# Token-mixing second weights loaded in two pieces, and the hand-kept instruction order replaced, in a two-layer attention and MLP kernel

## The chip, the cores and the metric

The kernel runs on one core of a Trainium2 chip. The metric is the device time of one execution in microseconds (us). TensorE (PE in the profile, its weight loads PEld), VectorE (DVE), ScalarE (ACT) and GpSimd (POOL) compute, SyncE (SP) issues nearly all DMAs. Every engine takes its own instructions strictly in the order in which they are written, and waits at semaphores for the others.

## The reference, cut to what matters

```python
x = x + A(layernorm(x), wqkv, wo)      # S = 2048 tokens, D = 512, 32 heads of 16
x = x + B(layernorm(x), w1, b1, w2, b2)
# both lines once more with the same weights: two layers

def A(x, wqkv, wo):                    # sliding-window attention, window W = 256
    q, k, v = heads(x @ wqkv)
    scores = q @ k.T * 16 ** -0.5, masked to 0 <= query - key < 256
    return softmax(scores) @ v, heads joined, @ wo

def B(x, w1, b1, w2, b2):              # the MLP mixes tokens, not features; F = 1792
    u = gelu(einsum("sd,sf->df", layernorm(x), w1) + b1)
    return transpose(u @ w2 + b2)      # [D, F] @ [F, S]
```

## The kernel before, in words

**Tiling.** x lies in SBUF as 16 tiles of 128 tokens by 512 features. Attention runs over four query blocks of 512 tokens (Q = 0 to 3). For a block, q, k and v are projected (four 128x512 products each, line 526, with the masking copies of lines 537 and 542 behind them), then four groups of heads (t = 0 to 3) with nine steps each (m = 0 to 8) follow. A step is a scores operation on TensorE (`emit_scores`, line 684: 4, 8 or 12 small 64x64 products), an exp on ScalarE (`emit_exp`, line 695), one or two small edge masks on VectorE or GpSimd (line 712), and a product with v (`emit_pv`, line 733, small products again). Probabilities go round through seven slots, the scores through two pairs of PSUM banks. After step 8 the sums are copied out (line 358 on VectorE, 360 on ScalarE) and DMAs bring the denominators together and add the second half of a pair of groups to `oU` (line 755); `job_inverse` and `job_normalise` (lines 757 and 767, a small-tile product at 777) divide, and `job_outproj` (line 648) multiplies with wo and adds to x.

**MLP.** The first product (`u_product`, line 849) runs over 14 tiles of F and 16 token tiles, in groups of four products (line 855). Its parts that need early tokens only are done inside attention. A gelu (line 903) makes the tile of `uT`. The second product (`job_y`, line 906) makes a token tile st of the output out of 14 products of 128x512 (line 928), in two operations of 10 and 4 products with one accumulation, and VectorE adds the result to x (line 932); the last tile of layer 2 is done in two halves of 256 columns (lines 915 and 919). In layer 1 the later of these products are laid between the steps of the second layer's attention; in layer 2 they come last, and each tile's output DMA follows its addition (line 940; 922 for the halves).

**The second weights.** A block s2 of w2 serves two token tiles and is 128 x 14 x 256 in bf16, 896 KB. `w2_dma` (line 845) loads it in one DMA into a home (`w2_place`, line 836): one of two slots of `w1buf`, or one of the two halves of `oU`. The load waits for every reader of the home, and each product waits for the whole block (`held`). Blocks 0 to 3 are loaded at the end of the first product, blocks 4 to 7 when `job_y` has used their home up (lines 935 to 938).

**What sets the order.** Every operation is a `plan.op` with its reads and writes, numbered as it is made. The five strings of `ORDER` give each engine its list of operations, two letters to a number: they fix both the sequence of each engine and, for operations that several engines can do, which does it. `BANKS` gives the PSUM bank (6 or 7) of each product that has no bank of its own. `arrange` (line 151) reads both; `needs` (line 199) works out which semaphores each operation has to wait for. SyncE's DMAs use 16 semaphores in turn, so that a DMA also waits for the one 16 places before it.

Of the kernel before, what the change touches and what calls it, by code (L numbers as in the profile page):

```python
# [29 lines left out]
AuAvAwAxAyAzBLBJA0BPBRBNBTBXBVDTB1CeCuA1A2CjCoBpCyCcC3C9D1A3CnDEDKCxBtC2DODXC8DkDDDeDJDNDmDVDbBxDsDxB5DBD4DiD9DrGsEKECDwEFFZD3EPD8EBEaEJGQEOETEjEeEyEp  # L30
EuGiE3EiE8EoEtFBE2FJE7FOF2FVFAFIFcFEFxFNFSF4HlF9FbGCFwGIF1F8GMGBGTHYGdGHGLGSGWGlICGpGvHLG2GkGoG9G7HCGuG1HGIQHOG5HBHFHVHNHSHeHaHiHrI0HyHdH6HhHqHxH-HuII
H5H+INKmIcIHIMIgIkIoIVIsKUIxIfIjI6JpI-IrIwJVH1JaI5I+JiJCJmJEJuJZJ1JfJyJ6JdKwJlJ+JtJxKLJ5LpKPJ9KXLbKhKKKOKpMFKtKWKaKzK-K6KoLBKsKyK5LGLPLKK9LFLSNILYLJLh
NSLmLRLVLuNLL1LgL9LlLdMCLtL0MKL8MBLxMJMOMPMdNBMlMhMWMpNwMtMgMkMxL4M5MsMwM+NgNEM4M9NNNQNXNDNdMSNKNnNUNtNaN1NcNmN5OOOGNsN0OKO+OTN4OFOJOeOQOXOiOnOpOhOtPm
O0OmO6NqPBOsOzPFM0O5PKPSQYPAPEPfPJPPPZPVPtPYPePjPNP4PyNkPcQAPiPsQHPoPxP3QRP-O3QGQbQKQVQoQkQUQaQfRXP7QvQeQ1Q-Q5QjQuQ0RDORRKQ4Q+RORHQERURcRRRNRhRTRbRgRm
RlRzR0QsSuR3R4R5SxSyS0SrS1SvS3SwSGS6S7SDS4S2SVSJSsSRSNS8S5StSlSmSzSnS9TRTFTBTNTSTHTDTOTdTVThTZTaTeTWSoTiSpSqS-TLTJT1TwT7T2T8UAUBTxUpUOUdUXUZUqUTUVUkU2
UbUeU6UlUiVbUPVMVCVKWdVVVQWeU+VeVjYXVGYYVoVvVUVsXyXzWiVdV0ViV4VnVuVzWAWNV9WPV3V-WHWEWyXRWZWUXAWlWLWqZgXBWvW3WTWYWkXkYrW8WpXNWuZWXWW2W7XGXbX7XgXVXaXfXp
YQXuX4aFYAXoYFXtZvYMX3X-YEYJYTaGYmYta2YyYSYlY3YqYxY8adZHZAa3Y2Y7Y-ZZZGZKZRbgZdZjZEbhZqZxZYcDZ2ZcZiZpZ6Zta-aCaNZ-Z1aaZ5aBaKaWaQaqaVaZajaia8apaxaSa7aybK
cGbFbdcHbZbEbJbSdRbqbucbbybNbcb7blcAambtbxcTb6b-cYdjcgcFcXckatcscdcweNc4cjcrc8bmdJcvc3c7dIdNdMdUb1eZdedmcndTdXdrczdxd4d9dld-dqdwd3eEgAeId7eQemeWeDeHef
duejePeTerfDeze7eeebeifAfIeqeyeufNe6e-fbfHfMfUfffjfngjfrfvfegXf3fifqfuf9e2gDf2gIiDgQf8gCgHgNgUh0gcgggLgogTgbgfgsfQg5gngrg9hchIg4hTfyg8hEhMhXheighChihp
hshthWhwh3hbhhhFh7hohviAiSiIh2h6iPhGiWh-iFiaiTikiOiVipiLiZivijioi3iuidi2i-i+jCjJjQjNkRjTjXjgj4jcjojMiyjujSjWjbjyjnjtjxj8jkj3kDkAkHjlkKkOkWi7kGkbkNkVka  # L40
kgkfktkui8kLkxkykzlrlslulolllmlvlplAl0lxk9l1lylPltlDlzlLlHl2lwlqlnlflglhmBl9l-mLl3mMmbmTmUmHl7mImcmPmQlimXljlkmYl5mFmDmjm1msmkmnmwmom2mxmtm5m6nCm+m-nH
# [25 lines left out]
ABAAACADAIAEAGAHAFCiCwDSCsC7CtDIDWDjGhGgG6EWEnHKEXEZEYGbGaGZGcHRDqK+KlKkGGIZLOIYIaIvIbKTKdKgKeKfMbMZMcMaOaOcOdObOWQNPwQPQnQOQQP2PrRfQiQzRyRkR8R9R+R-Q9
LkOlSjSiRGTuTvSkTlTmUDT4WMV8VZVaXDYaXLXJXKXMZuZ+ZUZVZPZNZOZQbVbYbWbXdid8dheMdpdadbdcddfXfZfYfahPf7hRhShQjGhLjFinjHjIitjahBj2jfkZiihakek4k2k3k5jsleksld
# [29 lines left out]
class Plan:  # L98
# [172 lines left out]
def bass_interleave_layers__sliding_block__mixer_token_mlp__prompt_kernel(  # L271
# [17 lines left out]
    NFT = F // P  # L289
# [5 lines left out]
    with es:  # L295
# [22 lines left out]
        uT = sb("uT", [P, NFT, D])  # L318
# [32 lines left out]
        def load(dst, src, size, prio, **kw):  # L351
            return plan.op({SP: (600, lambda e: e.dma_start(dst, src))}, prio=prio, dma=size, **kw)
# [553 lines left out]
        def job_y(st, b, L, prio):  # L906
            s2, last_layer = st // 2, L == 1
            blk, held = w2_place(L, s2)
            if last_layer and st == NT - 1:
                for h, bank in enumerate((b, b + 1)):  # L910
# [7 lines left out]
                    pe(f, 1530, prio, reads=held + [R("uT", fc) for fc in range(NFT)], writes=[BK(bank)])  # L918
# [6 lines left out]
            for lo, hi in ((0, 10), (10, NFT)):  # L925
                def f(e, lo=lo, hi=hi):
                    for fc in range(lo, hi):
                        r = e.matmul(ps[:, b, :], lhsT=blk[:, fc, (st % 2) * P:(st % 2 + 1) * P],  # L928
                                     rhs=uT[:, fc, :], start=(fc == 0), stop=(fc == NFT - 1))
                    return r  # L930
                pe(f, 217 * (hi - lo), prio, reads=held + [R("uT", fc) for fc in range(lo, hi)], writes=[BK(b)])
# [131 lines left out]
```

## Time and profile before

| | before |
|---|---|
| median of 3 runs (lowest, highest) | 492.09 us (491.19, 492.58) |
| the profiled execution itself | 492.09 us |
| its span, first to last instruction | 490.3 us |
| granted TensorE clock | 1.00 |
| TensorE busy | 467.3 us, 95% of the span |
| ScalarE busy | 319.8 us, 65% |
| VectorE busy | 337.4 us, 69% |
| GpSimd busy | 196.3 us, 40% |
| SyncE DMAs (instructions of `sync`) | 178 |

Stages, as the lines of the timeline show them: layer 1 attention to about 160 us, its first MLP product to 202 us, second MLP product to 224 us and then mixed into the attention of layer 2, which ends at about 396 us; first MLP product to 438 us; second to 488 us.

A row of a group reads: line, engine, operation, written tile <- read tiles, shape, count | busy us, mean ns of one | idle us of the engine just before them and what ended most of it. A row of waits reads: who <- whom: us in total, times, longest us. A row of the timeline reads: start, length, engine, line, operation, count, and in brackets the idle time before it with what ended it. A row of a stretch reads: stretch, its length, then busy us and count for PE, PEld, DVE, ACT and POOL, the clock, the DMA share and GB/s. In the chain a piece reads: start, length, what. "issue" is idle time for which the profile shows no cause.

### The profile page before, as it was taken

To read this page: it belongs to the slowest core of one execution; us is meant where nothing else is said; L and a number is where in the kernel's file an instruction comes from. 1 tells how busy PE (TensorE), PEld (TensorE's weight loads), DVE (VectorE), ACT (ScalarE), POOL (GpSimd) and SP (SyncE) were. 2 spreads that over 40 slices of the span, in tenths; PEclk is the share of its full clock that TensorE was granted. 3 is DMA by queue.
4 is the path that set the end of the run, shared out by engine and by line. 5 is a ranking of instruction groups with operands and counts; after the bars stand their busy time and mean duration, and the time that the engine had idled before them with its cause. 6 is when DMAs were issued, how large, how long until landed. Compare 5 with 4: busy or idle time off the path is not lost.

```text
span 490.3 us, 17141 instructions
## 1 busy us (share of the span) xinstructions
PE 467.3 (95%) x7614; PEld 255.4 (52%) x7706; DVE 337.4 (69%) x710; ACT 319.8 (65%) x391; POOL 196.3 (40%) x362
## 2 busy tenths in 40 slices
PE   8989989999999999999999999999999999999997
PEld 6544555565555444444455555655556544444444
DVE  7999988988878550256878677999978745220214
ACT  5989989999989202404769898989999830440000
POOL 4989886444622210021439253645674220000000
DMA  7533159200105872240116300240020666080833
GB/s 215 100 77 90 40 115 97 70 6 25 50 6 153 237 175 76 75 132 19 31 16 170 51 27 4 39 101 8 24 70 4 197 188 171 0 226 19 228 107 118
DMA packets 83465, 43.58 MB, mean 89 GB/s; under 512 B 18752, under 2 KB 82368, under 8 KB 83392
## 3 DMA queue, kind: packets, MB, share of 16 engines
q1 hardware_dynamic: 79520, 42.48, 33.1%
q0 software_dynamic: 3872, 0.02, 1.8%
q8 instruction: 60, 0.98, 0.9%
q14 instruction: 13, 0.11, 0.1%
HBM read 32.51 MB, written 2.10 MB: 71 GB/s over the span
## 4 chain that ended last, share of the span: by engine, by line
PE 77%; DVE 14%; ACT 4%; issue 3%; POOL 1%; POOLq 0%
PE ps L855 19%; PE ps L928 18%; PE ps L526 12%; PE ps L684 11%; PE ps L733 9%; PE ps L653 4%; ACT p_sb L695 4%; DVE q_sb L537 2%; DVE stats L460 2%; DVE p_sb L712 2%; PE ps L777 1%; DVE v_all L586 1%; DVE x_sb L657 1%; DVE k_sb L537 1%; DVE oU L358 1%
## 5 line engine op out<-in xcount | busy, mean ns | idle before, releaser
L695 ACT ACTIVATE p_sb<-ps 128x1024 bf16<-128x1024 f32 (+8 forms) x288 | 260.8, 973 | 26.0 <-PE ps L684 23.8
L712 POOL TENSOR_TENSOR p_sb<-p_sb,edge 128x128 bf16<-128x128 bf16 (+2 forms) x225 | 107.5, 494 | 122.8 <-ACT p_sb L695 99.0
L684 PE MATMUL ps<-q_sb,k_sb 64*64 64x288 bf16 (+8 forms) x2816 | 106.4, 250 | 2.3 <-issue 1.3
L526 PE MATMUL ps<-xhT,wqkv 128*128 128x512 bf16 x335 | 86.2, 380 | 7.7 <-issue 4.7
L733 PE MATMUL ps<-p_sb,v_all 64*64 64x288 bf16 (+8 forms) x2816 | 89.5, 246 | 1.7 <-DVE oU L358 0.7
L684 PEld LDWEIGHTS ps<-q_sb,k_sb 64*64 64x64 bf16 x2816 | 53.1, 106 | 51.8 <-ACT p_sb L695 32.7
L733 PEld LDWEIGHTS ps<-p_sb,v_all 64*64 64x64 bf16 x2816 | 58.7, 107 | 15.4 <-issue 4.7
L928 PE MATMUL ps<-uT,w1buf 128*128 128x512 bf16 x270 | 62.6, 379 | 1.2 <-issue 0.8
L932 DVE SCALAR_TENSOR_TENSOR x_sb<-ps,b2col,x_sb 128x512 bf16<-128x512 f32 x31 | 22.2, 745 | 50.8 <-PE ps L928 50.7
L712 DVE TENSOR_TENSOR p_sb<-p_sb,edge 128x64 bf16<-128x64 bf16 (+2 forms) x175 | 44.4, 272 | 12.7 <-ACT p_sb L695 12.0
L526 PEld LDWEIGHTS ps<-xhT,wqkv 128*128 128x128 bf16 x376 | 30.5, 97 | 40.0 <-issue 5.6
L855 PE MATMUL ps<-xh_sb,w1buf 128*128 128x512 bf16 x175 | 43.4, 380 | 2.1 <-issue 1.3
L928 PEld LDWEIGHTS ps<-uT,w1buf 128*128 128x128 bf16 x280 | 26.6, 98 | 32.4 <-issue 1.1
L492 ACT ACTIVATE xh_sb<-x_sb,shift,rstd 128x512 bf16<-128x512 bf16 x9 | 7.1, 811 | 54.8 <-POOL shift L486 54.8
L460 DVE BATCH_NORM_STATS2 stats<-x_sb 128x6 f32<-128x512 bf16 x64 | 42.3, 680 | 0.3
L482 POOL TENSOR_TENSOR rstd<-vare,mhalf 128x4 f32<-128x4 f32 x15 | 15.7, 1047 | 54.4 <-DVE nmean L484 32.7
L537 DVE TENSOR_TENSOR q_sb<-ps,even 128x1024 bf16<-128x1024 f32 x30 | 36.4, 1214 | 1.3 <-PE ps L526 1.0
L537 DVE TENSOR_TENSOR k_sb<-ps,half 128x1024 bf16<-128x1024 f32 (+1 forms) x27 | 32.3, 1198 | 4.8 <-PE ps L526 3.5
L928 PE MATMUL ps<-uT,oU 128*128 128x512 bf16 x149 | 34.9, 379 | 0.3
L653 PE MATMUL ps<-wo_sb,oT 128*128 128x512 bf16 x114 | 30.1, 380 | 1.6 <-issue 1.0
L855 PE MATMUL ps<-xh_sb,k_sb 128*128 128x512 bf16 x125 | 29.6, 379 | 0.2
L855 PEld LDWEIGHTS ps<-xh_sb,w1buf 128*128 128x128 bf16 x192 | 17.1, 98 | 21.2 <-issue 2.4
(87 smaller groups left out, 457.8 us busy)
## 6 DMA issues: line engine op xcount, KB each, us to landing
w1buf<-in_B_w_dram SPq DMA_DIRECT2D x10, 896.0 KB
oU<-in_B_w_dram SPq DMA_DIRECT2D x6, 896.0 KB
w1buf<-in_B_w_dram SPq DMA_DIRECT2D x10, 512.0 KB
oU<-o SPq DMA_DIRECT2D x16, 256.0 KB
k_sb<-in_B_w_dram SPq DMA_DIRECT2D x16, 256.0 KB
xhT<-in_B_w_dram SPq DMA_DIRECT2D x8, 256.0 KB
q_sb<-in_B_w_dram SPq DMA_DIRECT2D x8, 256.0 KB
out_dram<-x_sb SPq DMA_DIRECT2D x15, 128.0 KB
```

The source lines that it names most:

```text
L460: dve(lambda e: e.bn_stats(stats[:, t, :], x_sb[:, t, :]), 690, prio, reads=[R("x", t)], writes=[R("stats", t)])
L482: pool(lambda e: e.tensor_tensor(rstd[:, sl], vare[:, sl], mhalf[:], op=ALU.pow), 1000, prio, reads=[R("vare", g), R("mhalf")], writes=[R( ...
L526: last = e.matmul(ps[:, b, :], lhsT=wqkv[:, c, c0:c0 + P], rhs=xhT[:, buf, c, :], start=(c == 0), stop=(c == 3))
L537: return e.tensor_tensor(dst, src.unsqueeze(2).to_broadcast([P, n, 2, w]), mask[:].unsqueeze(1).unsqueeze(3).to_broadcast([P, n, 2, w]), o ...
L653: last = e.matmul(ps[:, b, :], lhsT=oT[:, buf, t, i * P:(i + 1) * P], rhs=wo_sb[:, t, :], start=(t == 0), stop=(t == 3))
L684: last = e.matmul(ps[64 * c:64 * c + 64, 2 * half + r, 32 * i0:32 * i1], lhsT=k_sb[rows, ring, t, kb % 16, :], rhs=q_sb[rows, t, c, 32 * i ...
L695: latest[0] = plan.op({ACT: (170 + int(2 * (512 - c0) * 0.84), lambda e: e.activation(p_sb[:, slot, :, c0:512], ps[:, 2 * half:2 * half + ...
L712: return e.tensor_tensor(v, v, g, op=ALU.mult)
L733: last = e.matmul(ps[64 * r:64 * r + 64, B_O + (c ^ r), 32 * i0:32 * i1], lhsT=v_all[rows, col:col + 64], rhs=p_sb[rows, slot, r, 32 * i0: ...
L855: r = e.matmul(ps[:, b, :], lhsT=blk[:, n, (ft % 2) * P:(ft % 2 + 1) * P], rhs=xh_sb[:, 4 * g + n, :], start=(first and g == quarters[0] a ...
L928: r = e.matmul(ps[:, b, :], lhsT=blk[:, fc, (st % 2) * P:(st % 2 + 1) * P], rhs=uT[:, fc, :], start=(fc == 0), stop=(fc == NFT - 1))
L932: dve(lambda e: e.scalar_tensor_tensor(x_sb[:, st, :], ps[:, b, :], b2col[:, st:st + 1], x_sb[:, st, :], op0=ALU.add, op1=ALU.add), 750, prio,
```

## The change

- `w2_dma` loads a block in two DMAs: 8 of the 14 F tiles (512 KB) and 6 of them (384 KB). Each writes, and so waits for, only its half of the home.
- The two operations of a second product are cut at the same place, 8 and 6 products where it was 10 and 4, and each waits for its own piece only. The halves of the last tile wait for both.
- All five lists of `ORDER` and `BANKS` are new, since every later operation has a new number and the order was searched anew.

Decoded and matched one to one, the tables of both hold the same operations but for the 16 added loads. The lists have these lengths before and after: tensor 916 and 916, vector 710 and 707, scalar 375 and 375, gpsimd 358 and 361, sync 178 and 194. More than 250 operations change their engine, most of them edge masks of line 712 (96 from GpSimd to VectorE, 94 the other way). On TensorE most operations move by a few places within the same stage. The last operations of layer 2 were tile 14, the two halves of tile 15, then tile 13; now they are the second half of tile 15, then tile 14, then the first half of tile 15.

```diff
-    "tensor": "AuAvAwAxAyAzBLBJA0BPBRBNBTBXBV ...
+    "tensor": "AuAvAwAxAyBLAzBJA0BPBNBTBRBVBX ...
...
-                return flat[:, 0:NFT * 256].rearrange("p (f s) -> p f s", f=NFT), [R("w1", k, h) for h in range(2)]
+                return flat[:, 0:NFT * 256].rearrange("p (f s) -> p f s", f=NFT), [[R("w1", k, h)] for h in range(2)]
...
-            return (flat[:, 0:NFT * 256].rearrange("p (f s) -> p f s", f=NFT), [r for t in range(4) for r in held_o(k - 2, t)])
+            return (flat[:, 0:NFT * 256].rearrange("p (f s) -> p f s", f=NFT),
+                    [[r for t in (2 * h, 2 * h + 1) for r in held_o(k - 2, t)] for h in range(2)])
+
+        W2_PARTS = ((0, 8), (8, NFT))

         def w2_dma(L, s2, prio, after=()):
             dst, held = w2_place(L, s2)
-            load(dst, w2v[:, :, s2 * 256:(s2 + 1) * 256], 7 << 17, prio, reads=after, writes=held)
+            for h, (lo, hi) in enumerate(W2_PARTS):
+                load(dst[:, lo:hi, :], w2v[:, lo:hi, s2 * 256:(s2 + 1) * 256], (hi - lo) << 16, prio, reads=after, writes=held[h])
...
-                    pe(f, 1530, prio, reads=held + [R("uT", fc) for fc in range(NFT)], writes=[BK(bank)])
+                    pe(f, 1530, prio, reads=held[0] + held[1] + [R("uT", fc) for fc in range(NFT)], writes=[BK(bank)])
...
-            for lo, hi in ((0, 10), (10, NFT)):
+            for part, (lo, hi) in enumerate(W2_PARTS):
...
-                pe(f, 217 * (hi - lo), prio, reads=held + [R("uT", fc) for fc in range(lo, hi)], writes=[BK(b)])
+                pe(f, 217 * (hi - lo), prio, reads=held[part] + [R("uT", fc) for fc in range(lo, hi)], writes=[BK(b)])
```

More of the change, by code (lines that the diff above doesn't have):

```diff
@@ L34 @@
[L34 to L41, printed above, removed]
@@ new lines @@
+NILhNSLmLuNLL1LgLlLdL9LtMCL0L8MKLxMBMPMJNBMdMhNwMOMpMlMtMWMxL4M5MgMkMsM+MwM4NENQNNM9NXNgNdNDNKNUNnNaNtNcN1MSN5NmNsN0OGOOOKN4OTO+OeOFOJOQOiOXOnOpOtPmOh
+O0OmOsO6NqPBOzO5PFM0PKPAPSQYPZPEPfPJPPPVPjPtNkPNPYPyPeP4PcPiPsQAQHPoPxP3P-QRO3QGQVQKQbP7QoQfQkRXQvQUQaQeQ1Q-Q5QjQuRDORRKQ0Q4ROQsRUQ+RHRcQERhRNRTRbRmRg
+RlRzR0RRSuR3R4R5SvSrSsS3S0S4SxSGS1S2SDS6S5SRSJSySVS7SNSwStSoSlSzSpSmSqTHSnTDTFTBTZS9S8S-TaThTNTVTOTiTRTSTWTdTeTLTJT0UFT5UGT1T6UAUBUqUUUvUZUjUfUrUdUbUk
+VQU8UVUhUoUwVAVEVSVIWjWkVMVWVbYeVpVkYfVhVuV1VaX5X6VyV6VjVoV+VtV0V5WGWTWoV9WNWFWVWDW4WfWaWKXYXGWRWwWrXHWZW1WeW9WqWvW0XCZoW8XBXNXUXdXrYzXiXnZeYCXwXcX1Xh
@@ new lines @@
+XmXvX0X-YXYMYHaNZ3YTYaX+aOYuYGYLYQY1a+Y6YZY-Yta-ZEZIYyY5Y+ZDZPalZZZHZOZSZhboZrZlZMbpZyZgZ5cLZ+ZkZqZxaCbHaKZ1aVaHZ9aiaBaJaSaeaYayadarahbEaqaaaxa6a5bDbS
+cObNbldZbMbhcPbybRb2babVb6cjcDbkbtb1cIb5aucbcCcHcgdrcocNcfcsa1c0clc4eVdAcrczdEbudRc3c-dDdQdVdUdcb9ehdmdbduc7dzdfeFd5eAcvdteHdyd4d-eMgIeQeDeYeueeeLeneP
+eXeberd2ezfLe7emfDejeqfIeye6fCfQe2fVfHfPfUfcfjfrfnfvgrfmfzfqfyf3gff-f2gFe+gLf+gEgQiLgYgKgPgcgVh8gkgogTgbgwgjgngvg0fYhBgzhFf6hQhkhbhAhfiohEhmhMhKhqhxhU
+h0h1h4heh-hjhNhpiDhwh3iIiaiQh+iCiXiHiNiehOiiibisixiWiTidihi3iriwi2i-ili+jGjKjHjRjYkZjVjUjbjojfi6jkjajejwkAj2jjj6jskEjvj1kLjtkPj5j-kWjDkIkejEkjkOkVkdko
@@ new lines @@
+kiknk1k2kSkTk5k6k7lwl8l5lzl2l9l6lIltlulFl3lxlXlPl0lLlTlylvl1l4lqlrlsl7mHmJmBmPmjmDmQmFlnmTmkmblomXmfmgmUmcmYl+lpl-mLmNmzm9m+mvnDnEm5m6mwnHnIm0nNnbnjnf
+nRnOnknSnXngnrnnnsncnonYn2nvnwnz""",
+    "vector": """
+AcAdAeAWAfAUAgA5A7A6A8BBA-A9BAA+BFBEBDAQAhAaBIBHBKBbBOBdARBcBfBZBSBaAVBeBgAnBhBjAYCvAXAbAZBrCgBsB4BoCdChD2FgC1C-FmBvFkBwFiAtBzFlFjFnFhJJFoB6B0DdDcDzGt
+JFFqD-DpB7DvD7EAD0FvFaB8JHGREVElEREHESEIEgE+EmE-E5GjEsEhFDE0F3FFFUJIE1FzFGF0HmFHHnGOHZGPJKGYGXJLHoIEJGGxJMHMGyJPG4JNIRG8ISGzI1HUHQHJHgHTHkHcHbH0HvH8Hw
@@ new lines @@
+H9KnITIlIXIWKVIeIqI2JqIzImH2InJrH3JXJDJYJsJ2J3JoJhJ4H4J0JeJ8KCKxJwKAKEI4LqKIKRLcKZKSKBKjKcKbLALrK1K8LQLWMGK2LMNJNTLXNMLaLwLjLfLeL-LsLzLyNCNxMfNyMRMNMr
+NzMYMXMvL5MmL6MHNRM8MzMnNhL7NVNWNbMIMTN3NiNjMUMoOPOMO-N9OgN-MVOZOoPnOrOCOwOxNrM1O9QZOBPWPXPRM2PbPOPhPdP6PpPqQJO4QLQMQXP8P9QdQCQDQTRYQpQqQrQhRAQ3QyOSRB
+QtP+RIRJRZRCRoRpRaRsRqRSR6R7RxQFRvSASCSHSISFSESSSKSWSXSTSOSLSPSMSQSUSYSZSbSfSgTbTPTjTTTXTfUHT7UKT2T+T3UCT-ULUDT4UEUOUMUaUTUgUeUcUsU9UlU+UmUiUnUWUxUtVC
+VFUyVGUXWlUuUzUYVNU0VLVYVOU2VeVVYgYjVmVnU4ViV3VxVrX7V4WmVzWAWUWpWJV8WEW5WnWXWMW6W7X8XaWPWYYkX9WcWQXIW3XLXbZpXMYlXWXPY0XEXtXXXlXFZfXpXyYDYYX3YnYBYsYqXq
@@ new lines @@
+YpZ4YPYEYSYVYRY3YxaPY4Y8Y9bAZBZKZUbBanZTZNbqZuZtbCZncMZ7ZvbrZ8aAaFaIaUaXaTaZatacbJa0bGaba8aQdacQbncRbUb0aRbsbccSbWckbXcTawcGavcVcddscicqbYcucncma2cXc6
+a3bvdCcZeWdHbwdTb+b-eidgc8dXeGd1c9cwd7gJd8eveSeweTecedd3fMe1ekelfFexe4e3fda4fSbxfXfefNfscxgsfxfOgtggcyghfte-c+dIgugHiMgXgWgefAdKfugigUh9fBdMg4fZdNfag6
+f7g3hlhHhSg-iphhg+hdhVhohshLhziBhtfbh7iOhuiPhPiciSiViUizi5iminjBjLjCjZkajpkbjTf8jqi7i8j8j4jrkBjukCi9kckDkKkukskYkgjFkqk4k8kUlClDlElJlKlGlHlYlQlRlZlUlS
+lMlalVlWlNlOlbldlhmRmlmhmVmdmZnFm7m-mxnJm1nlnTnPntnhnZndn3npnxn0""",
+    "scalar": """
@@ new lines @@
+AjAlBMBQBUBWBYDUB2CfBqCkCpAoCzC4C+DFBuDLDPDYByDfDnDlDtDyDCD5D+EDELEGEbEQEqEkEUE4EvEfE9FCEzFKFPFWFdFTFyF5F+GDGJGNGUGeGmGqIDGwG3G+HDHHHPHWHfHjHsHzH7IAIJ
+IOIdIhIpItIyI7JAJWJbJjJnJvJzJgJ7J-KMKQKYKiKqKuK0K7LCLHLLLTLZLiK3LnLvL2L+MDMLMQMeMiMqMuMyM6M-NFNONYNeNoNuN2N6OHOLOUOfOjOYOqOuO1O7PCPGPLPTPaPgPkPQPuNlPz
+P5QBQIQSQWQcQgQlQwQ2Q6A4RERLRPRVRdRiRnR1RuShSBRwSdSeTETCTITGS+TATcTkTQTUTYTgTKTMUQVRUpVBVTVJVHVcVXVlVqVvVPV2V7V-WHWOWWWgWbWLXZWsWxW2W+XDXVXeXsXjXOXoXx
+X2YAYIYNYrYUYbYvY2YFZAY7ZFZJZQZaZiamZmZsZzZ6Z-aDbIaWaLajafazasbFa7bTbKbObmbibzb3bbb7cEcJccchcpctc1c5dBdFdSdWdddndvd0dhd6eBeIeNeReZefd9eoese0e8fEfJfRfW
@@ L66 @@
+WITpWBWhWiWtWyWdWzWuYmXfW-XAXkXgXzTrX4YoYOYJXuYcYwYKYdYWTtZCZGZjaoZLapZRZbZ0aEZwaMakagbLbPa9bjbQb4b8cFbZcUcKcec2cWdGcYcacBdodwdYdecAeJeKeOeCepd+eaeget
+e9fGfKfTflfpf1f5gBgCgNdJgSgOgadLdOgmdPg5gygqg2g7g9hIg8hDh6iFiGhviKiZikigiui0jJjhjXjdf9jyjmjzkNkRj9kGktkvkykxklkrkzlclelflg""",
     "sync": """
[L67 to L68 removed]
```

40 lines of the change are left out of this document (12 added, 28 removed).

## The prediction

> **What bounds it now.** I read the shares of the engines first, then the chain, the rows of the second product, TensorE's waits, the stretches of attention, and last the timeline around the longest gaps. The page, sections 1, 4 and 5:
>
> ```profile
> PE 467.3 (95%) x7614; PEld 255.4 (52%) x7706; DVE 337.4 (69%) x710; ACT 319.8 (65%) x391; POOL 196.3 (40%) x362
> ...
> PE 77%; DVE 14%; ACT 4%; issue 3%; POOL 1%; POOLq 0%
> ...
> L928 PE MATMUL ps<-uT,w1buf 128*128 128x512 bf16 x270 | 62.6, 379 | 1.2 <-issue 0.8
> ...
> L928 PE MATMUL ps<-uT,oU 128*128 128x512 bf16 x149 | 34.9, 379 | 0.3
> ```
>
> The longest of TensorE's waits:
>
> ```profile
> PEld ps L684 <- ACT p_sb L695: 32.7, 83, 0.5
> ```
>
> TensorE is busy for 95% of the span and carries 77% of the chain that ended last. The two rows of the second product (L928) are the first finding on the change: in 419 records TensorE sat idle 1.5 us before them, and no DMA is named. **No product waits for a w2 load before the change**, so the split has no stall to remove. What TensorE does wait for is in attention: 83 times its weight loads of the scores wait for an exp.
>
> Stretches, of attention and of the last second product:
>
> ```profile
> 12.00:30.00 18.00, 16.23 (x270) 9.13 (x266) 17.88 (x44) 16.76 (x26) 16.81 (x36) 1.00 0.48 105
> 300.00:340.00 40.00, 38.01 (x988) 23.11 (x996) 36.15 (x69) 37.02 (x41) 22.69 (x37) 1.00 0.21 44
> 431.30:433.30 2.00, 2.00 (x11) 0.92 (x10) 1.29 (x2) 1.57 (x4) 0.00 (x0) 1.00 1.10 327
> 433.30:435.30 2.00, 2.00 (x11) 0.88 (x9) 0.00 (x0) 1.23 (x3) 0.00 (x0) 1.00 1.19 290
> ```
>
> Columns: busy time of PE, PEld, DVE, ACT and POOL, then the clock, the DMA share and GB/s. In attention PE and ACT are both over 90% busy, and from 12 to 30 us DVE too: order and engine choice decide there, and a gain for one shows up against another.
>
> The timeline of SP, and of TensorE around three gaps:
>
> ```profile
> 23.68 0.47 SPq L352 DMA_DIRECT2D wo_sb<-in_A_wo_dram  x1
> 24.19 1.19 SPq L507 DMA_TRANSPOSE xhT<-xh_sb  x1
> ```
>
> ```profile
> 29.30 0.56 PEld L526 LDWEIGHTS ps<-xhT,wqkv 128*128 128x128 bf16 x4 [1.23 <-ACT p_sb L695]
> ...
> 65.77 0.27 PE L684 MATMUL ps<-q_sb,k_sb 64*64 64x256 bf16 x1 [1.35 <-issue]
> ...
> 135.37 0.39 PEld L733 LDWEIGHTS ps<-p_sb,v_all 64*64 64x64 bf16 x20 [0.86 <-DVE oU L358]
> ```
>
> Only nine gaps over 0.2 us have neither PE nor PEld at work, 5.1 us together; the three above are the longest. The one at 29.30 is put down to an exp, but the product's own ScalarE operand was done at 27.9; it also reads the transposes of block 1, and of the last one's 16 landings, 14 came by 27.31 and the last two at 28.05 and 29.24. So a DMA ended it.
>
> **The change, part by part.** The profiled execution took 492.09 us, its span 490.3; that is the median of the three runs, so sums start at 492.09.
>
> *Loads in two.* The same bytes, 16 more issues on SP. The w2 issues took 0.37 to 0.85 us each when not held back by their queue, so 6 to 14 us more of SP, which is idle most of the span. The largest risk is at the end of layer 2. There the second piece of block 1 is the third of three 384 KB loads, the first let go when operation 877 of TensorE's list ends; seven groups of four (0.86 each) and two pieces of eight (1.73 each) are to come before its use: 9.5 us. Before, the first load at 429.27 brought 86 GB/s for two microseconds and then 290 to 330: 1.18 MB take 1.5 + 4 + 0.5 = 6 us. 3.5 us remain. The same count for the first pieces of blocks 4 and 5 leaves some 2 us. Value 0.
>
> *Products 8 and 6.* The same 14 weight loads and matmuls, one accumulation. 0.
>
> *Order on TensorE.* The trace, read by weight-load starts, prices a change between full products and small-tile work: a group of four full products takes 0.86 in a row of its like and 0.97 alone between small-tile operations (L526, 60 of them), and a scores operation of 12 takes 0.35 before a full product, 0.21 before small-tile work. One excursion is worth 0.11 + 0.14 = 0.25. The tables have 266 such changes before and 270 after: two excursions more, **+0.5**.
>
> *The tail.* The last operation was a whole tile's second part, with an addition of 0.75 (L932) and 128 KB out behind it. Now it is half a tile: 0.48 (L919) and 64 KB. -0.27, and at 290 GB/s some -0.2 at most for the bytes, of which I take -0.1 as other outputs are still under way: **-0.4**.
>
> *The gap at 29.30.* Block 1's transposes become SP's issues 12, 13, 15 and 16, ahead of both wo loads; before, the last was the 18th, behind an x load (0.58) and a wo load (0.47). It can go about 1.1 us sooner. The product that needs it moves four places up, worth some 0.6. With 14 of 16 landings as the measure the gap goes, with the two stragglers it only halves. **-1.0**, ends -0.5 and -1.0.
>
> *The gap at 135.37.* The first product with v of a group waits for both copies of the sums before. It now stands behind another scores, a group of four and a q projection, 2 us of work, and one copy moves to ScalarE. **-0.7**, ends 0 and -0.7. Next late there is the exp two steps on.
>
> *The gap at 65.77.* Both waits of its neighbours had ended by 64.4. Instruction packets of 16 KB come on queue q8 about every 128 matmuls; that one began 80 matmuls after its turn, at 63.3, and ended at 64.4. I read it as a late fetch, which either kernel may meet anywhere: 0, ends -1.35 and +1.35.
>
> The Trainium skill, "Runtime: NRT & Kernel Launch", section Instruction fetch mechanics, says the opposite: instructions are fetched ahead in 16 KB blocks and the cost is mostly hidden. The trace has the blocks (60 packets of 16 KB) but also the 1.35 us. By that rule the gap would be the order's own and could go with it; its time is a rival below.
>
> *Engine choice.* Each operation that changes engine is priced by the mean of its kind on the other engine in this trace, in the stretch where it stood. ScalarE gets +1.3 from 12 to 30 us, -1.0 to 60, +0.3, +0.6 and +0.3 to 176, -2.3 from 226 to 260, -0.3, +1.5 (300 to 340), +0.3 and +0.2: +0.9 in all. VectorE loses 2.1, GpSimd gains 3.6, off the path for the most. ScalarE also waits itself for scores, 23.8 us in all, so I take half: **+0.5**, ends 0 and +0.9, and more in the rival.
>
> *One wait that may be new.* At the end of layer 1's attention the DMA that brings half of the sums to `oU` now has two 256 KB loads ahead of it. It landed at 165.4 and its reader ran at 168.0; 512 KB at 290 GB/s are 1.8 us, and the reader comes one group of products (0.86) sooner. About 0; ends 0 and +1.0.
>
> *Everything else that is shuffled.* The six other gaps are 2.1 us in sum, and the first, 0.65, is the start-up chain. They may go or be replaced: 0, ends -2 and +2.
>
> Sum: 492.09 + 0.5 - 0.4 - 1.0 - 0.7 + 0.5 = **491.0 us**, 0.2% less. A difference under 0.3% (1.5 us) can't be told from none here: below 490.6 is faster, above 493.6 slower.
>
> **Rivals.**
> - *The new order closes layer 1's small waits too* (faster). From 12 to 140 us PE is busy 119.5 of 128 us, 93.3%; from 300 to 380 it is 75.8 of 80, 94.7%, with the same kind of work. If layer 1 came to layer 2's share: 1.4% of 128, 1.8 us more, 489.2. For: three of the four longest gaps lie before 140 us. Against: the distance from scores to their product with v, in PE work, is the same in both tables (median 4.6 and 4.5 us in layer 1).
> - *The fetch gap is the order's and goes* (the rule above): 491.0 - 1.35 = 489.7. Against: the fetch that ended as it began.
> - *ScalarE takes over* (slower). From 12 to 30 us it has 1.2 us idle and gets 1.3 more; from 300 to 340, 3.0 idle and 1.5 more. It decides once its idle time is less than what its exps need between scores. Then both additions count whole, and the gap at 29.30 is covered by exps: 492.09 + 0.5 - 0.4 + 1.3 + 1.5 = 495.0. For: both gaps on TensorE would then be paid anyway. Against: more is taken than given from 226 to 260.
> - *The pieces come late* (slower). If each piece cost a landing of 2 us one after the other, the three loads above would take 3 x 2 + 4 = 10 us against 9.5, and the third load of the next group, needed after 9 us, 10.8: with one more such place some 3 us in sum, 494. Against: 327 and 290 GB/s over three loads before, with no dip between them.
>
>   The Trainium skill, "DMA: Bandwidth & Descriptors", section Rules for kernel authors, advises against splits: 1 MiB and more per DMA, small ones joined. By its fixed 2 us per DMA the sum would be this rival's; the trace shows such starts overlapped.
>
> **How the numbers follow.** Forecast 0.38 (within 0.3%), layer 1 closed 0.24, fetch gap gone 0.12 (both faster), ScalarE 0.22 and late pieces 0.04 (both slower). So faster 0.36, same 0.38, slower 0.26. From the forecast the ends of the unknown costs reach about 3 us each way; to 488.0 it takes in both faster cases with a further microsecond, to 495.0 the ScalarE case. The forecast's own range is 490.6 to 493.6.
>
> **What would show it.** No idle time named DMA before L928; 16 more w2 issues, 512 and 384 KB; last addition L919, 0.48; no gap of 1 us before L526 near 29 us nor 0.7 before L733 near 135; 60 instruction packets. Wrong if L928 waits for a w2 load, if ACT's busy share from 12 to 30 us nears 18.0, or if the layers' spans shift by over 3 us.

## The result, and the profile after

The changed kernel took 489.70 us (median of 11 runs, 488.76 to 491.12), the kernel before 491.87 us in the runs beside them (490.94 to 492.62): a ratio of **0.9956, 95% interval 0.9944 to 0.9968**, or 2.2 us less. The forecast was 491.0 us, a gain of half that size, in a range of 488 to 495.

The profiled execution of the changed kernel took 490.92 us, with a span of 489.2. Lines behind 850 are four further on: the second product's L928 is now L932 and its addition L936, the halves' products are L919 (they were L915) and their addition L923 (it was L919). The kernels of the experiments shift a few lines more: L527 there stands for L526, L685 for L684, L734 and L736 for L733, L929 for L928. The page, sections 1, 4 and 5:

```profile
PE 480.0 (98%) x7706; PEld 255.4 (52%) x7706; DVE 335.3 (69%) x707; ACT 319.7 (65%) x391; POOL 199.6 (41%) x365
...
PE 91%; ACT 5%; DMA 1%; DVE 1%; SPq 1%; issue 0%
...
L932 PE MATMUL ps<-uT,w1buf 128*128 128x512 bf16 x280 | 64.3, 380 | 0.0
...
L932 PE MATMUL ps<-uT,oU 128*128 128x512 bf16 x154 | 35.5, 380 | 0.0
```

No product waits for a w2 load, as before. The steps from 95% to 98% of busy time and from 77% to 91% of the chain are for the most no gain: the profile of before holds 7,614 matmul records for 7,706 weight loads, this one all of them. The first experiment below has TensorE's order of before with every record (83% of its chain are PE's), and its page reads

```profile
PE 480.8 (98%) x7706; PEld 256.6 (52%) x7706; DVE 338.4 (69%) x710; ACT 319.9 (65%) x391; POOL 196.8 (40%) x362
```

in a span of 492.0. So PE's busy shares of the pages before and after can't be compared; the starts of the weight loads can, and all that follows goes by them. The prediction's comparison of the layers by these shares, 93.3% and 94.7%, falls with it: with every record, the old order has 97.7% and 98.3% there ("loads only" below). The scores' waits for exps (83 times 32.7 us before) are as they were in sum, and the stretches show ScalarE busier:

```profile
PEld ps L684 <- ACT p_sb L695: 32.9, 83, 0.6
```

```profile
12.00:30.00 18.00, 17.85 (x258) 9.40 (x259) 17.19 (x44) 17.66 (x29) 16.66 (x40) 1.00 0.58 132
300.00:340.00 40.00, 39.95 (x989) 23.10 (x987) 35.71 (x73) 37.77 (x44) 20.85 (x36) 1.00 0.15 32
...
433.30:435.30 2.00, 2.00 (x11) 0.92 (x10) 1.08 (x2) 2.00 (x4) 0.00 (x0) 1.00 1.00 285
```

ScalarE went from 16.76 to 17.66 us in the first stretch and from 37.02 to 37.77 in the second, +0.9 and +0.75 where the working had +1.3 and +1.5. The first comes close to the 18.0 that the prediction named as a sign of being wrong, but TensorE did not pay for it: from 10.6 to 47.6 us it gains (table below). TensorE's timeline at the three gaps the prediction showed:

```profile
28.04 1.41 PEld L526 LDWEIGHTS ps<-xhT,wqkv 128*128 128x128 bf16 x8 [0.18 <-ACT k_sb L542]
...
64.61 0.51 PEld L777 LDWEIGHTS ps<-rc,spread 64*64 64x64 bf16 x32
...
135.90 0.23 PEld L684 LDWEIGHTS ps<-q_sb,k_sb 64*64 64x64 bf16 x12 [0.41 <-ACT p_sb L695]
```

The projection waits 0.18 where it waited 1.23; the small products of line 777, which stood behind the 1.35 us, follow without a wait; and near 135 us neither PE nor PEld works for 0.21 us where it was 0.67.

**Where the time went.** TensorE's two orders have done exactly the same operations at 369 places, so the two traces can be laid side by side there. The table gives the start of the same operation minus its start in the profile of before, in us; "old" and "new" say whose order stands up to there. The kernels are those of the experiments.

| | 10.6 | 47.6 | 66.2 | 82.9 | 141.9 | 200.3 | 298.5 | 393.8 | 456.5 | PE's end |
|---|---|---|---|---|---|---|---|---|---|---|
| loads only (old) | 0.01 | -0.45 | -0.92 | -0.92 | -0.91 | -0.92 | -0.92 | -0.90 | -0.90 | -0.90 |
| cut only (old) | 0.22 | 0.68 | -0.10 | 0.22 | 0.25 | 0.25 | 1.65 | 1.95 | 1.95 | 1.95 |
| split, old order | 0.21 | 0.20 | -0.39 | -0.08 | -0.05 | -0.05 | 1.40 | 1.70 | 1.70 | 1.70 |
| new to 152 | 1.17 | -0.52 | -1.49 | -1.45 | -0.95 | -0.98 | 0.43 | 0.73 | 0.73 | 0.73 |
| new from 152 | 0.22 | 2.87 | 2.65 | 2.65 | 2.66 | 2.92 | 2.65 | 1.83 | 1.83 | 2.04 |
| changed (new) | 1.46 | -0.10 | -1.08 | 0.04 | 0.55 | 0.51 | 0.24 | -0.58 | -0.58 | -0.37 |

Up to 142 us the same order differs from profile to profile by an event or two; behind that its steps repeat to some hundredths. The new order gains 0.27 us from 200 to 298, 0.82 from 298 to 394 (the same 0.82 in "new from 152"), loses 0.21 in the last products and gains 0.76 behind them. Before 142 us it gains and gives back. The changed kernel's profile is one of its longer runs, 490.92 us against a median of 489.70, while that of before lies near its median; the places before 142 us are where its runs can differ.

### The profile page after: what moved, and what is told of

Same layout as the page of the kernel before. It is cut to its first block, busy times and chain, and to the rows that moved or that the text cites. A ratio compares the mean times of both kernels' runs of the same rounds, so it can differ in the third digit from the quotient of the medians.

```text
span 489.2 us, 17263 instructions
## 1 busy us (share of the span) xinstructions
PE 480.0 (98%) x7706; PEld 255.4 (52%) x7706; DVE 335.3 (69%) x707; ACT 319.7 (65%) x391; POOL 199.6 (41%) x365
## 4 chain that ended last, share of the span: by engine, by line
PE 91%; ACT 5%; DMA 1%; DVE 1%; SPq 1%; issue 0%
PE ps L859 20%; PE ps L932 19%; PE ps L526 17%; PE ps L684 14%; PE ps L733 12%; PE ps L653 6%; ACT p_sb L695 4%; PE ps L777 1%; DMA x_sb<-in_A_x_dram 1%; PE ps L919 1%; SPq L352 1%; PE ps L446 0%; DVE o L358 0%; DVE q_sb L537 0%; ACT vT L360 0%
## 5 line engine op out<-in xcount | busy, mean ns | idle before, releaser
L712 POOL TENSOR_TENSOR p_sb<-p_sb,edge 128x256 bf16<-128x256 bf16 (+2 forms) x223 | 106.8, 494 | 102.7 <-ACT p_sb L695 88.0
L684 PE MATMUL ps<-q_sb,k_sb 64*64 64x288 bf16 (+8 forms) x2816 | 107.2, 250 | 1.4 <-ACT p_sb L695 1.1
L526 PE MATMUL ps<-xhT,wqkv 128*128 128x512 bf16 x376 | 95.6, 382 | 0.2 <-DVE q_sb L537 0.2
L733 PE MATMUL ps<-p_sb,v_all 64*64 64x288 bf16 (+8 forms) x2816 | 89.7, 246 | 1.6 <-DVE o L358 1.1
L684 PEld LDWEIGHTS ps<-q_sb,k_sb 64*64 64x64 bf16 x2816 | 53.6, 106 | 53.4 <-ACT p_sb L695 32.9
L733 PEld LDWEIGHTS ps<-p_sb,v_all 64*64 64x64 bf16 x2816 | 58.4, 107 | 14.8 <-issue 5.5
L932 PE MATMUL ps<-uT,w1buf 128*128 128x512 bf16 x280 | 64.3, 380 | 0.0
L936 DVE SCALAR_TENSOR_TENSOR x_sb<-ps,b2col,x_sb 128x512 bf16<-128x512 f32 x31 | 22.6, 745 | 51.0 <-PE ps L932 50.9
L712 DVE TENSOR_TENSOR p_sb<-p_sb,edge 128x256 bf16<-128x256 bf16 (+2 forms) x177 | 45.3, 275 | 14.1 <-ACT p_sb L695 12.7
L526 PEld LDWEIGHTS ps<-xhT,wqkv 128*128 128x128 bf16 x376 | 30.6, 98 | 39.7 <-issue 5.4
L859 PE MATMUL ps<-xh_sb,w1buf 128*128 128x512 bf16 x192 | 46.3, 381 | 0.0
L932 PEld LDWEIGHTS ps<-uT,w1buf 128*128 128x128 bf16 x280 | 26.3, 98 | 32.3 <-issue 1.3
L537 DVE TENSOR_TENSOR k_sb<-ps,half 128x1024 bf16<-128x1024 f32 (+1 forms) x29 | 34.7, 1197 | 5.0 <-PE ps L526 4.9
L537 DVE TENSOR_TENSOR q_sb<-ps,even 128x1024 bf16<-128x1024 f32 x29 | 35.3, 1217 | 1.9 <-PE ps L526 1.5
L932 PE MATMUL ps<-uT,oU 128*128 128x512 bf16 x154 | 35.5, 380 | 0.0
L653 PE MATMUL ps<-wo_sb,oT 128*128 128x512 bf16 x128 | 32.4, 381 | 0.0
L859 PE MATMUL ps<-xh_sb,k_sb 128*128 128x512 bf16 x128 | 30.8, 380 | 0.0
L586 POOL TENSOR_TENSOR v_all<-vB,v_all 128x512 bf16<-128x512 bf16 (+1 forms) x16 | 23.5, 1474 | 16.8 <-DVE vB L601 16.6
```

The source lines that it names most:

```text
L526: last = e.matmul(ps[:, b, :], lhsT=wqkv[:, c, c0:c0 + P], rhs=xhT[:, buf, c, :], start=(c == 0), stop=(c == 3))
L537: return e.tensor_tensor(dst, src.unsqueeze(2).to_broadcast([P, n, 2, w]), mask[:].unsqueeze(1).unsqueeze(3).to_broadcast([P, n, 2, w]), o ...
L586: return e.tensor_tensor(d, src.unsqueeze(2).to_broadcast([P, k, 2, DH]), v_all[:, 0:32].rearrange("p (h d) -> p h d", h=2).unsqueeze(1).t ...
L653: last = e.matmul(ps[:, b, :], lhsT=oT[:, buf, t, i * P:(i + 1) * P], rhs=wo_sb[:, t, :], start=(t == 0), stop=(t == 3))
L684: last = e.matmul(ps[64 * c:64 * c + 64, 2 * half + r, 32 * i0:32 * i1], lhsT=k_sb[rows, ring, t, kb % 16, :], rhs=q_sb[rows, t, c, 32 * i ...
L712: return e.tensor_tensor(v, v, g, op=ALU.mult)
```

## The experiments

**The split in the old order.** The old lists renumbered, each second piece right behind the first on SP.

> The kernel before with loads in two and products cut 8/6, all its five lists and its banks kept; the second piece stands right behind the first on SP. Forecast's theory (no product waited for a load, so the split itself is worth nothing): 491.9 us, within 0.3% of before, and no idle time named DMA before the second product. Rival (the split pays, since a product starts on the first piece): 489.7 us, the time of the changed kernel. Second rival (late pieces): 494 us.

Measured: 493.68 us, ratio 1.0029 (1.0014 to 1.0044). None of the three theories: slower by 1.5 us, and since no DMA is named before the second product, late pieces are not the cause, near as 494 lies. By the starts of the same operations it is lost from 214 to 242 us (1.09), near 285 (0.33) and near 304 (0.28). The next two ask which half of the edit does it.

**The loads alone.** Two pieces, products still cut 10 and 4, both waiting for both pieces.

> Old order, loads in two pieces of 512 and 384 KB, but products still cut 10/4, each waiting for both pieces. Theory (it is the cut, not the loads, that cost 1.5 us in the old order): 492.0 us, as before, with the layer norm's copies for the transposes near 219 us as early as before. Rival (the 16 more issues or the smaller transfers cost it): 493.6 us.

**The cut alone.** The kernel before with one line changed.

```diff
-            for lo, hi in ((0, 10), (10, NFT)):
+            for lo, hi in ((0, 8), (8, NFT)):
```

> The kernel before with whole loads and the old order, only the products of a second product cut 8/6 instead of 10/4. Theory (the cut moves the ends of the products in an order that was laid out for 10/4): 493.6 us, with the idle time of 0.67 us before the transposes near 219.7 us that the kernel with both had. Rival (the loads cost it): 492.0 us.

Measured: loads only 491.21 us, 0.9984 (0.9968 to 1.0001); cut only 493.24 us, 1.0034 (1.0019 to 1.0050). So the loads in two cost nothing, and **the cut costs the old order 1.6 us**. TensorE at the transposes behind layer 1's second product, first before, then with the cut:

```profile
220.62 0.65 PEld L515 LDWEIGHTS ps<-ident,xh_sb 128*128 128x128 bf16 x8
```

```profile
220.62 0.23 PEld L515 LDWEIGHTS ps<-ident,xh_sb 128*128 128x128 bf16 x4 [1.17 <-ACT xh_sb L492]
```

Three first parts stand ahead of these transposes and their second parts behind. With parts of 8 TensorE comes 0.4 us sooner for each of these, and waits for the layer norm's xh, which comes when it came; the longer second parts still follow in full.

**The new order on whole loads.** The lists of the change on the code of before, each load at the place of its second piece.

> The new lists and banks on the code of before: whole loads, products cut 10/4, each load at the place of its second piece. Forecast's theory (the order is the whole gain): 489.7 us, as the changed kernel. Rival (the split pays): 491.9 us. Between: if the new order leans on the first pieces in the last second product, some of L928's products wait for a load there, up to 1.5 us a wait, 490 to 493 us, with DMA named before L928.

Measured: 513.2 us, 1.0432 (1.0405 to 1.0459), far beyond my "between" case. TensorE's waits name the loads:

```profile
PEld ps L929 <- DMA w1buf<-in_B_w_dram: 16.7, 4, 5.9
```

Four waits, two in each layer's second product, where a first part stands early in the new list and its block, as a whole, is let go with the second piece.

**The new order with the old cut.** The changed kernel, products cut 10 and 4, waiting for both pieces.

> The changed kernel with loads in two, but products cut 10/4, both waiting for both pieces. Theory (each order is laid out for its own cut, as the old one lost 1.5 us with 8/6; and its first products start on their first piece): 491 to 495 us, with DMA named before L932's products. Rival (the new order does not need the cut): 489.7 us.

Measured: 502.62 us, 1.0214 (1.0191 to 1.0236), beyond the range that was given. TensorE's timeline, then the stretch behind that wait:

```profile
468.35 0.13 PEld L932 LDWEIGHTS ps<-uT,w1buf 128*128 128x128 bf16 x2 [8.77 <-DMA w1buf<-in_B_w_dram]
```

```profile
468.30:474.30 6.00, 5.95 (x15) 2.11 (x16) 0.00 (x0) 0.00 (x0) 0.00 (x0) 0.50 0.00 0
```

One first part in the last second product waits 8.8 us for its second piece, and behind it the clock is still granted at 0.50 for 6 us, where a matmul starts every 0.43 us and not every 0.22. A second wait for a piece, 0.9 us, stands near 270 us. This kernel changes the cut and the waits together, so what the old cut alone would cost the new order is not shown. The new order does use the split: it lets the second pieces go late and starts products on the first. That buys no time by itself, since the old order had no wait there.

**The two halves of the order.** Split code; the lists change over where operation 362 of TensorE's list is reached, 152 us.

> Split code; new order and engines up to the operation at which 362 of TensorE's list are done (152 us in the profile of before), the old order from there. Forecast's steps (gap at 29.30 -1.0, gap at 135.37 -0.7, half of ScalarE's +1.2 in that stretch): 490.8 us. Rival, from the two profiles alone (the changed kernel is 0.6 us behind at 138 us and gains 1.8 after): 492.4 us. Second rival (the profile's late start is chance, the layer gains 1.0 behind it): 490.9 us, with the first 13 us as in before.

> The mirror image: old order and engines to the same point, the new ones from there, split code. Forecast's steps (tail -0.4, ScalarE about 0, changes of mode +0.3): 491.8 us. Rival, from the two profiles alone: 490.1 us. If the parts add up, this gain and that of the kernel that is new up to 152 us sum to the 2.2 us of the whole.

Measured: new up to 152 us 493.11 us, 1.0019 (1.0001 to 1.0037); new from 152 us 490.27 us, 0.9967 (0.9950 to 0.9985). My numbers for the first forgot that it keeps the old order, and so the cost of the cut, behind 152 us. Against the split in the old order (1.0029) it gains 0.1%, which alone is not clear of the noise, the other 0.6%; from 1.0029 both together give 0.9957, the changed kernel's 0.9956. The parts add up well within their intervals, and **three quarters or more of the gain come from behind 152 us**. The rival from the two profiles read that part rightly (490.1). For the part before, its 492.4 owes its nearness to two errors: it too left out the cost of the cut, and it had 0.6 us lost where this kernel's profile is 0.95 us ahead at 142 us. (The 2.6 us that "new from 152" lies behind by 40 us stand in its old part, where its profile has a gap of 1.93 at 28.57 and a clock of 0.94 from 30 to 60 us.)

**The transposes first.** The kernel before, one stretch of SP's list.

```diff
-  transpose 2, transpose 0, load x, transpose 1, load x, load wo, transpose 3
+  transpose 2, transpose 0, transpose 1, transpose 3, load x, load x, load wo
```

> The kernel before, where SP issues the four transposes of block 1 together, ahead of the two x loads and the wo load that stood between them; nothing else is changed. Forecast's step (a late transpose ends the gap at 29.30): the gap of 0.95 us goes or halves, 491.1 to 491.6 us. Rival (an exp ends it, as the profile puts it): the gap stays, 492.0 us.

Measured: 491.37 us, 0.9994 (0.9985 to 1.0003). The gap is gone. SP's and TensorE's timeline:

```profile
19.09 5.76 SPq L508 DMA_TRANSPOSE xhT<-xh_sb  x3
```

```profile
28.78 0.55 PEld L527 LDWEIGHTS ps<-xhT,wqkv 128*128 128x128 bf16 x4 [0.18 <-issue]
```

The exps were not touched, so a late transpose ended that gap, though the profile names an exp. The landings say the same: in all seven profiles that have the gap, it ends 0.05 to 0.06 us after the last of the fourth transpose's 16 landings (29.24 and 29.30 before). A late block of instructions, the cause of the gap in the next experiment, is not it here: such a block lands 1.07 to 1.24 us before the end of the gap in six of the seven profiles, but 2.15 us in the seventh, and in this kernel one lands at 29.04, when the projection has long begun. From 10.6 to 40 us TensorE gains 0.81 by the trace; the median shows 0.3, with an interval that reaches from 0.7 less to 0.15 more.

**The instruction stream shifted.** The kernel before, with the twelve projections of block 1 in layer 1 done in halves of columns. These projections do not hold the reference's sums here; all other operations and their order are those of before.

```diff
+                cols = 256 if Q == 1 and prio < 300 else 512
...
+                    for a in range(0, 512, cols):
+                        last = e.matmul(ps[:, b, a:a + cols], lhsT=..., rhs=xhT[:, buf, c, a:a + cols], ...)
```

> The kernel before, where the twelve projections of block 1 in layer 1 (TensorE's operations 56 to 123, 30 to 55 us) are each done as eight products of 256 columns instead of four of 512: 48 more pairs of weight load and matmul ahead of the gap at 65.77, so that each 16 KB instruction packet behind them is asked for 48 pairs earlier in the order of the work. Theory (the gap is a late fetch: in six profiles with the old order it ends 1.22 to 1.45 us after a packet that is asked for 28 to 52 pairs after its turn): the gap goes or falls under 0.2 us, worth 0.9; the split products cost 0.2 to 0.6 of it, 491.1 to 491.9 us. Rival (the gap belongs to the operations that stand there, as their wait for an exp or a copy): it stays at 0.6 to 1.35 us, 492.0 to 492.6 us.

Measured: the gap at 65.77 is gone, and from 58 to 66 us TensorE gains 1.27. The time is 494.03 us, 1.0036 (1.0024 to 1.0048), 2 us over what I gave. Two gaps like it stand elsewhere (PE's timeline of this kernel):

```profile
104.17 0.45 PE L736 MATMUL ps<-p_sb,v_all 64*64 64x32 bf16 x12 [0.59 <-issue]
...
340.71 0.30 PE L736 MATMUL ps<-p_sb,v_all 64*64 64x256 bf16 x4 [0.57 <-issue]
```

I shifted every packet behind 55 us, not one. These two cost 0.78 each by the starts, and a copy at 82 us (below) 0.6. The mechanism is shown by the times. In each kernel the 16 KB packet on queue q8 that landed last before the gap:

| kernel, place | packet landed | gap | its end after the landing |
|---|---|---|---|
| before | 64.41 | 64.42 to 65.77 | 1.36 |
| split, old order | 64.06 | 64.63 to 65.38 | 1.32 |
| loads only | 63.64 | 64.03 to 64.86 | 1.22 |
| cut only | 64.33 | 65.11 to 65.68 | 1.35 |
| transposes first | 63.90 | 64.19 to 65.29 | 1.39 |
| new from 152 | 66.97 | 67.32 to 68.42 | 1.45 |
| engines only | 64.77 | 64.80 to 66.15 | 1.38 |
| stream shifted | 102.79 | 103.58 to 104.17 | 1.38 |
| stream shifted | 339.27 | 340.13 to 340.71 | 1.44 |
| three parts | 64.09 | 65.03 to 65.58 | 1.49 |
| three parts | 390.94 | 391.90 to 392.42 | 1.48 |

Where the gap begins changes, where it ends does not: 1.2 to 1.5 us after the packet. I read it so that TensorE has used up what it had and waits for the next block; why a packet is asked for late is not shown. The old order has this gap near 65 us in all seven profiles that leave the stream as it was; the new order has it there in one of six ("three parts"), where the packet was asked for at 62.99 and not, as in the other five, between 60.7 and 62.1.

**The engines alone.** The kernel before with its own sequence on TensorE; the 74 operations between 298 and 396 us that change engine go to the new one.

> The kernel before with its own sequence on TensorE, but the 74 operations that run between 298 and 396 us and have another engine in the new tables go to that engine, each at the place that its old start gives. Theory A (the 0.82 us that the new order gains from 298 to 394 us, alike in three profiles, comes from the choice of engines, that is from masks and copies that come in time): 491.1 us and no gaps before L733 near 322 and 374 us. Theory B (it comes from the sequence on TensorE together with the engines, neither alone): 491.9 us or slower. The forecast's ScalarE term (the time that ScalarE is given counts half): 492.5 us.

Measured: 497.51 us, 1.0107 (1.0089 to 1.0124). Theory A is out: 4.8 us are lost from 298 to 394 us, where sequence and engines of the change together gain 0.82. The new engines do not fit the old sequence. Theory B is shown for this half alone: the new sequence with the old engines was not run, and the moved operations stood where their old starts put them, which may be part of the 4.8. TensorE's waits in that stretch, first with the engines alone, then in "loads only" (the old order with every record), then in the changed kernel:

```profile
PEld ps L685 <- ACT p_sb L696: 10.1, 23, 1.1
...
PEld ps L734 <- POOL p_sb L713: 2.6, 3, 0.9
PEld ps L527 <- DVE vT L359: 1.7, 2, 1.0
```

```profile
PEld ps L685 <- ACT p_sb L696: 10.1, 24, 0.4
...
PEld ps L734 <- DVE p_sb L713: 2.0, 4, 0.8
```

```profile
PEld ps L684 <- ACT p_sb L695: 8.3, 21, 0.4
```

The old order waits four times, 2.0 us, for masks of VectorE; in the changed kernel that row is gone, and the exps are waited for 1.8 us less although ScalarE is busier there (91.02 of 96 us against 88.52).

**A better mixture.** Two tries to drop what the new order loses: the old start (30 operations, 19 us), and the old order from 83 to 142 us.

> Old order for the first 30 operations of TensorE (19 us) and what precedes them, the changed kernel's from there. Theory (the changed kernel's start is 1.0 us slower in its own right: 1.17 and 1.46 us behind at 10.6 us against 0.2 with the old start): 488.7 us, 1 us under the changed kernel and faster than both. Rival (what is late at the start is waited for anyway by 47 us, where loads or exps set the pace): 489.7 us.

> The changed kernel, but with the old order and engines for TensorE's operations 188 to 338 (83 to 142 us), where the new order loses 1.15 us up to 118 us and gets 0.67 back, alike in three profiles. If the parts add up: 489.2 us, 0.5 us under the changed kernel and faster than both. Rival (the seams cost more than the stretch gives, as with the old start): 489.7 us or slower.

Measured: old start 490.78 us, 0.9988 (0.9976 to 1.0000); three parts 491.42 us, 0.9982 (0.9966 to 0.9998). Both ratios lie above the change's 0.9956, which is from another session. (The one profile of "old start" is 0.6 us shorter than that of the change, which is one of its longer runs.) The first one's seam has a gap of its own, 1.30 us at 19.85, in which a projection waits for VectorE. The second meets a fetch gap in each of its outer parts, and this (ScalarE's timeline):

```profile
83.00 0.60 ACT L361 ACTIVATE o<-ps 128x512 f32<-128x512 f32 x1 [1.28 <-DMA oU<-o]
```

The same copy in the changed kernel, on VectorE:

```profile
82.18 0.69 DVE L358 COPY o<-ps 128x512 f32<-128x512 f32 x1 [1.56 <-PE ps L526]
```

The profile names a matmul there, but ScalarE had copied the neighbouring sums at 80.73. The copy also waits for the DMAs that still read `o`. SP's timeline of the changed kernel:

```profile
76.57 0.59 SPq L352 DMA_DIRECT2D oU<-o  x1
77.20 0.58 SPq L352 DMA_DIRECT2D w1buf<-in_B_w_dram  x1
77.84 1.39 SPq L507 DMA_TRANSPOSE xhT<-xh_sb  x1
79.28 0.69 SPq L352 DMA_DIRECT2D den_c<-o  x1
```

The first, 256 KB and the one that "three parts" waits for, had landed here at 79.09. The last, 8 KB of denominators, stands behind a 512 KB load and a transpose and landed at 82.10; the copy begins 0.08 us later, as it does in all five kernels that have the new order in this place. On the clock of before (by the differences at 66.2 us) that landing comes at 82.1 and 82.0 in "new to 152" and "old start", which lose nothing from 66.2 to 82.9 us, and at 83.2, 83.2 and 83.6 in the change, "new order on whole loads" and "new order with the old cut", which lose 1.1, 1.1 and 1.5 us. This is read from profiles; no experiment moved these DMAs.

## Why the prediction held, and where its sum was wrong

Its sign and range held, and its order of causes did not. That the sum came within 1.3 us is in part luck: the late start (+1.46 in the changed kernel's profile) and the stall at 82 us (+1.1), neither of which it had, take back about what the gaps at 29.30 and 65.77 give. Step by step:

- *Loads in two, 0.* Right: 0.9984 (0.9968 to 1.0001) alone, and no wait at L932. The count of 9.5 us against 6 for the pieces held (the first load went out at 432.14, the third landed at 438.10, its product began at 441.23); the rival of late pieces is out for this order. The Trainium skill, "DMA: Bandwidth & Descriptors", section Rules for kernel authors, asks for 1 MiB and more per DMA for the highest bandwidth; here 512 and 384 KB in place of 896 KB cost nothing.
- *Products 8 and 6, 0.* **Wrong as a cost of the cut by itself**, right for the kernel as changed. I counted instructions only. In the old order the cut costs 1.6 us, by its effect on when TensorE reaches the next wait; the new order is laid out for it (0.27 gained in that stretch).
- *Gap at 29.30, -1.0.* The cause (a transpose) is shown. From 10.6 to 47.6 us the five profiles with the new start gain 1.56 to 1.71 us on the profile of before, more than this gap; but they come into this stretch late (next point).
- *Start-up, counted among the six other gaps at 0.* **Missed.** In the new order TensorE reaches the place of 10.6 us 0.8 to 1.8 us later in five profiles, against 0 to 0.5 in nine with the old. It takes back what the transposes give. In the changed kernel's profile two waits stand there, 0.69 us to 9.40 and 0.65 us to 11.32, both put down to VectorE's copies of the transposed tokens (`xhT`, L358); the profile of before has no gap over 0.2 us there.
- *Gap at 135.37, -0.7.* It shrank from 0.67 to 0.21, and from 134 to 142 us the new order gains 0.42. The working's "next late there is the exp" is what the row at 135.90 shows.
- *Gap at 65.77, 0, "either kernel may meet it anywhere".* **The step of a cause rightly seen and wrongly valued.** It is a late fetch, but it belongs to a place of an order: 0.57 to 1.35 us in seven of seven. The new order is spared it mostly, and from 47.6 to 66.2 us gains 1.0 in five profiles and 0.3 in the sixth, against 0 to 0.8 with the old. The rival "the fetch gap goes" (489.7) was right about this gap, and its agreement with the measured time is chance: the gap is one term of several. The Trainium skill, "Runtime: NRT & Kernel Launch", section Instruction fetch mechanics, has the next block fetched while one is executed and the crossing mostly hidden; 16 KB blocks agree, and the eleven gaps of 0.5 to 1.35 us above are crossings that were not hidden.
- *Engine choice, +0.5.* **Wrong sign for the stretch that pays most.** From 298 to 394 us ScalarE got more and TensorE 0.82 us less to wait. The step priced engines apart from the sequence; "engines only" shows that they can't be: in the old sequence they cost 4.8 us. The rival "ScalarE takes over" is out.
- *Order on TensorE, +0.5.* Not tested alone, and the table does not set it apart.
- *One wait that may be new, 0.* Right: from 142 to 200 us the table moves by 0.04, though the last part of that DMA landed at 168.38 (165.96 before, where the working has 165.4).
- *The tail, -0.4.* Right in kind: VectorE's last addition before and after is

```profile
487.15 0.75 DVE L932 SCALAR_TENSOR_TENSOR x_sb<-ps,b2col,x_sb 128x512 bf16<-128x512 f32 x1 [1.49 <-PE ps L928]
```

```profile
486.57 0.48 DVE L923 SCALAR_TENSOR_TENSOR x_sb<-ps,b2col,x_sb 128x256 bf16<-128x256 f32 x1 [0.78 <-PE ps L919]
```

  From the end of TensorE's last weight load to the end of the span it was 3.70 us and is 2.94, but TensorE's last products take 0.21 more: -0.55.
- *Everything else shuffled, 0, ends -2 and +2.* **This is the mis-sized term.** Three of its six gaps (322.38, 373.87, 374.95, 0.90 us together) went, about the 0.82 from 298 to 394 us. I had counted them among the six and given them no price. The rival "layer 1 closed" is not borne out: at 142 us the changed kernel's profile is 0.55 us behind.

In sum: behind 152 us -0.27 - 0.82 - 0.55 = -1.6, measured alone as 0.9967 of 492.1, also -1.6. Before it, by the ratios, about -0.5, in which the late start, the transposes, the fetch gap and the stall at 82 us nearly cancel. How often that stall and the fetch gap come in unprofiled runs stays open, and with it the split of those 0.5 us.

## What to carry to other kernels

An order worked out for given sizes of its pieces is part of those sizes: change a cut or an engine under an old order and it can lose several times what the edit is worth, so edit and order have to be tried together and each alone. Short gaps that the profile puts down to "issue" or to an operand long done deserve a price in a forecast: look for an instruction packet that landed 1.2 to 1.5 us before the gap's end, or for a DMA, however small, on another operand. Where two orders have done the same set of operations, compare their traces there and splice them at such a place: here the parts added up, though a seam can bring a wait of its own.

## What the runs showed of the hardware

- Late instruction blocks stop TensorE for 0.5 to 1.35 us, and the stop ends 1.22 to 1.49 us after the 16 KB packet lands, eleven times out of eleven. Adding 48 pairs of instructions moved the places.
- TensorE's granted clock fell to 0.50 during or just behind long gaps and stayed there for 3.4 us or a multiple. A gap of 1.93 us ("new from 152", 28.57 to 30.50) was enough: 0.50 from 30.7 for 3.4 us. In "new order with the old cut" it was at 0.50 from 464.1, 4 us into the long wait, to 474.4, 6 us behind it; those 6 us at half speed cost some 3. No gap up to 1.42 us lowered it in any profile, the late fetches included.
- Of the 16 parts of one DMA transpose, the last landed 1.2 to 1.5 us after the one before it in six of the seven profiles with the gap at 29.30 (28.05 and 29.24 before), and the reader waited for that one.
- A copy of 8 KB inside SBUF, issued behind a 512 KB load and a transpose, landed 2.8 us after its issue (79.28 to 82.10, the changed kernel); the 256 KB copy ahead of that load took 2.5 us (76.57 to 79.09).
